# Cached-attention decode, two layers: eight instead of seven value quarters kept per row, and the first small loads issued by ScalarE

## The chip, the cores and the metric

The kernel runs on one core of a Trainium2 chip. The metric is the device time of one launch in microseconds (us). The engines are PE (TensorE: matmuls and transposes), DVE (VectorE), ACT (ScalarE), POOL (GpSimd) and SP (SyncE, which here only issues transfers). Sixteen DMA engines move data between HBM and the on-chip memory.

## The reference

Eight rows (one new token each) pass twice through attention over a long cache and an MLP. The weights and the cache are the same in both passes.

```python
# B = 8 rows, D = 448, 16 query heads on 8 cache heads, Sk = 4096, Dh = 256, bf16
def _A_ref(x, k_cache, v_cache, wq, wo):
    q = (x @ wq) split into heads
    k = jnp.repeat(k_cache, rep, axis=1)
    v = jnp.repeat(v_cache, rep, axis=1)
    scores = jnp.einsum("bhqd,bhkd->bhqk", q, k) * (Dh ** -0.5)
    p = _softmax(scores, axis=-1)
    o = jnp.einsum("bhqk,bhkd->bhqd", p, v)
    return heads of o side by side @ wo

def _B_ref(x, w1, w2, w3, w4):
    ...
    h2 = _gelu(_layernorm(x1, axis=-1) @ w3) @ w4
    return x1 + h2

x = A_x
x = x + _A_ref(_layernorm(x, axis=-1), A_k_cache, A_v_cache, A_wq, A_wo)
x = x + _B_ref(_layernorm(x, axis=-1), B_w1, B_w2, B_w3, B_w4)
x = x + _A_ref(_layernorm(x, axis=-1), A_k_cache, A_v_cache, A_wq, A_wo)
x = x + _B_ref(_layernorm(x, axis=-1), B_w1, B_w2, B_w3, B_w4)
```

The keys and the values of one row and one cache head are 4096 x 256 numbers of 2 bytes, 2 MiB each. All keys and values together are 268 MB, and each is used in both layers.

## The kernel before, in words

**The cache in quarters.** A head's 4096 positions are laid on 128 partitions, 32 positions on each. A *quarter* is a fourth of them: 8 positions a partition, 4096 bytes a partition, 512 KB. The tile `kv` (line 502) has room for 30 quarters (`QUARTERS`, line 14), its *slots*. A transfer brings one to four neighbouring quarters of one head into as many neighbouring free slots (`issue_kv`, line 640; the issue itself is line 646), so it has 512, 1024, 1536 or 2048 KB.

**What happens to a quarter.** Keys: PE transposes a quarter in two pieces into PSUM (line 1510), DVE or ACT copies each piece back over the slot (lines 1441 and 1442), and PE multiplies it with the queries, in one of two forms (lines 1149 and 1406). Values: PE multiplies the softmax weights with the quarter (line 1276, in `pv`), eight matmuls. The last reader of a slot carries `o.frees` (lines 1184, 1215, 1217 and 1298): only then may SP issue a transfer into that slot.

**What stays for the second layer.** Row by row, layer 0 of a row is followed by its MLP and by layer 1 of the same row, so a part of the row's keys and values can stay in the slots and is not loaded twice. `KEEP_K` (line 22) is 5: the keys of heads 3 to 6 stay whole, in 16 slots. Of head 7 (`HALF`) one quarter stays in a slot and the other three in PSUM banks and a side buffer (`hold` and `half_piece`). `KEEP_V` (line 23) is 7: the four value quarters of head 7 and quarters 1 to 3 of head 6 stay (`KEPT_V`, line 1102). So 24 slots of 30 are held at the most, and six go round. Heads 0, 1 and 2 are the *free heads*, of which nothing stays.

**The crossing.** This is the text's name for the stretch of a row in which all that is kept is held: from the last layer 0 load of the row (head 7's values) until layer 1 has scored the first kept keys, whose slots then come free. In it runs the chain of small steps that leads from one layer to the next: the output projection, the MLP, the normalisation and the new queries (`mid`, line 1540). Meanwhile SP loads the values of the next row's free heads, whose softmax weights are already there, as transfers of one quarter each (`MOST` = 1, line 39), and PE uses them up (lines 1688 and 1689 of the main loop). Behind them come values of layer 1's heads 6, 5 and 4.

**The order of the work.** Every step is recorded as an operation with an engine, an estimated duration and what it reads and writes (`Plan.op`, line 113). A planner (`Plan.schedule`, line 160) then fixes the order on every engine before anything runs. It assumes a latency of a transfer and a rate, chooses the slots and how many quarters go in one transfer (`next_kv`, line 206), puts filler matmuls (line 1719) where it sees PE idle, and so gives another order when a constant changes. SP issues strictly in its order: one transfer whose slot is not free holds up all behind it.

**The start.** `dma_once` (line 632) records transfers on SP. The rows `x_row` come first, then half of `wqx_sb` and half of `w3x_sb` (the last 64 rows of wq and of w3, folded on two halves of the partitions), then the first keys and wq. The other halves are issued on ACT's queue (lines 1576 and 1580). SP's place for a transfer is its last argument or `prio`; keys and values are numbered 0, 1, 2 and so on, so the numbers 0, 0.05 and 0.06 (times 4, less 0.5) stand ahead of all of them.

**The end.** The last value quarters are used by `pv_turned` (line 1286), and 28 columns of two rows pass the MLP (`last_rows`, line 948) to the last two output transfers (line 983).

Of the kernel before, what the change touches and what calls it, by code (L numbers as in the profile page):

```python
# [6 lines left out]
P = 128  # L7
B = 8
D = 448
# [10 lines left out]
RSQRT_STEPS = ((0.703952253, 1.681914091), (0.5, 1.5000003))  # L20
RSQRT_F = RSQRT_STEPS[1][0] * RSQRT_STEPS[0][0] ** 3
KEEP_K = 5
KEEP_V = 7
HOLD = 2
MARGIN4, MARGIN2 = 6, 2
REP = 24
# [450 lines left out]
def bass_interleave_layers__gqa_block_cached__mixer_s_mlp__decode_kernel(  # L477
# [20 lines left out]
    plan = Plan()  # L498
# [6 lines left out]
    def sb(name, shape, dt):  # L505
        n = 4 if dt in (f32, i32) else 2
        for s in shape[1:]:
            n *= s
        al = 32 if n >= 128 else 8
        cursor[0] = (cursor[0] + al - 1) // al * al  # L510
        t = nc.alloc_sbuf_tensor_at(name, shape, dt, offset=cursor[0], align_bytes=al)
        cursor[0] += (n + al - 1) // al * al
        assert cursor[0] <= high0, (name, cursor[0], high0)
        return t

    wq_sb = sb("wq_sb", [P, 3, 4096], bf)
    wqx_sb = sb("wqx_sb", [P, 2048], bf)
    wo_sb = sb("wo_sb", [P, 32 * D], bf)
    w3_sb = sb("w3_sb", [P, 3, F], bf)
    w3x_sb = sb("w3x_sb", [P, F // 2], bf)  # L520
# [40 lines left out]
    def over(name, shape, dt, at, skip=0):  # L561
        return nc.alloc_sbuf_tensor_at(name, shape, dt, offset=at.manual_sbuf_range[0] + skip)
# [13 lines left out]
    x_row = over("x_row", [B, NC5 * P], bf, w4_sb)  # L576
# [49 lines left out]
    def dma(name, dst, src, nbytes, sem, val, wr, at, row=8192):  # L626

        us = nbytes / 16 / 26.88e3 + nbytes / row / 16 * 0.008
        plan.op("sp", lambda eng: eng.dma_start(dst, src), us / FASTER, name, wr=wr, prio=at,  # L629
                dma=(sem, val))  # L630

    def dma_once(name, parts, keys, at, also=()):

        for i, (dst, src, nbytes, *row) in enumerate(parts):
            dma(name, dst, src, nbytes, nc.alloc_semaphore(f"s_{name}{i}"), 16,
                [keys[i], *(also if i == 0 else ())], 4 * at - 0.5, *row)
# [49 lines left out]
    def const_c(v):  # L686
# [7 lines left out]
            wr=["sel"])  # L694
# [7 lines left out]
    for bank, key in [(psR, "R"), (psM, M)]:  # L702
        plan.op("dve", lambda v, bank=bank: v.memset(bank[:, :], 0.0), 0.5, "const",
                wr=["psM", ("row", 0), ("row", 1)], banks=[key])
# [396 lines left out]
    lent = {}  # L1101
    KEPT_V = {HKV - 1 - i: range(max(4 * i + 4 - KEEP_V, 0), 4) for i in range((KEEP_V + 3) // 4)}
    done = {}
# [452 lines left out]
    def second_queries(b, h, prio):  # L1556
# [8 lines left out]
           rd=["psM", ("mom2", b), "cs_q"], wr=[("q2", b % 2, h)], banks=[M], prio=prio)  # L1565


    dma_once("x", [(x_row[:, 0:D], A_x[:, 0, :], 7168), (x_row[:, D + P:], A_x[:, 0, 3 * P:D], 1024)],
             ["xr0", "xr1"], 0)

    def load_wq():
        dma_once("wq", [(wq_sb[:, kc, :], A_wq[kc * P:(kc + 1) * P, :], 1 << 20)
                        for kc in range(3)], ["wq0", "wq1", "wq2"], 2)
        dma_once("wqx", [(wqx_sb[0:64, :], A_wq[384:D, 0:2048], 1 << 19)], ["wqx0"], 0.05)
        s_wqx = nc.alloc_semaphore("s_wqx1")
        plan.op("act", lambda a: a.dma_start(wqx_sb[64:P, :], A_wq[384:D, 2048:4096]), 0.1, "wqx1",
                wr=["wqx1"], prio=0, dma=(s_wqx, 16))
        dma_once("w3x", [(w3x_sb[0:64, :], B_w3[384:D, 0:896], 114688)], ["w3x0"], 0.06)
        s_w3x = nc.alloc_semaphore("s_w3x1")
        plan.op("act", lambda a: a.dma_start(w3x_sb[64:P, :], B_w3[384:D, 896:1792]), 0.1, "w3x1",  # L1580
                wr=["w3x1"], prio=1, dma=(s_w3x, 16))

    def load_rest():
        dma_once("wo", [(wo_sb[:, :].rearrange("p (t n) -> p t n", n=2 * D),
# [68 lines left out]
    def with_first_results(k, b):  # L1653
# [15 lines left out]
        run(k[MLP_TO:])  # L1669

    load_wq()
    load_rest()
    first_queries()
# [105 lines left out]
```

## Time and profile before

| | us |
|---|---|
| median of 3 runs | 1074.54 (1074.22 to 1076.17) |
| profiled execution | 1071.74 |
| its span, first to last instruction | 1069.8 |
| PE busy | 937.8 |
| DVE busy | 586.8 |
| ACT busy | 345.6 |

The mean granted PE clock is 0.954 of full speed. HBM read is 434.18 MB, 406 GB/s over the span. The profile's page cuts the span into 40 slices of 26.7 us and gives for each the busy share of every engine in tenths, the granted clock (PEclk), the busy share of the DMA engines (DMA) and the rate. A row of the batch takes about 128 us, so one crossing comes every five slices or so.

In a line such as `SPq L646 <- PE psP L1276` the queue of SP waited at the instruction of line 646 until PE had finished the one of line 1276 that writes the tile psP; the numbers are the sum of such waits, how many there were, and the longest. A line on DMA issues gives what is loaded from where, the number of issues, the size of each and the median time from issue to landing. A row of a table by stretches has the stretch, its length, and for each engine the busy time with the number of instructions, then the granted clock, the DMA share and the rate.

### The profile page before, as it was taken

To read this page: it belongs to the slowest core of one execution; us is meant where nothing else is said; L and a number is where in the kernel's file an instruction comes from. 1 tells how busy PE (TensorE), PEld (TensorE's weight loads), DVE (VectorE), ACT (ScalarE), POOL (GpSimd) and SP (SyncE) were. 2 spreads that over 40 slices of the span, in tenths; PEclk is the share of its full clock that TensorE was granted. 3 is DMA by queue.
4 is the path that set the end of the run, shared out by engine and by line. 5 is a ranking of instruction groups with operands and counts; after the bars stand their busy time and mean duration, and the time that the engine had idled before them with its cause. 6 is when DMAs were issued, how large, how long until landed. Compare 5 with 4: busy or idle time off the path is not lost.

```text
span 1069.8 us, 34153 instructions
## 1 busy us (share of the span) xinstructions
PE 937.8 (88%) x15215; PEld 650.7 (61%) x15215; DVE 586.8 (55%) x1879; ACT 345.6 (32%) x946; POOL 99.6 (9%) x284
## 2 busy tenths in 40 slices
PE   4889889998989989988898888898888998998896
PEld 4556556665556656666565565666656675666664
DVE  4345455555555556555565555565555665665464
ACT  1234113341334502354133431344223342253041
POOL 0000000010100101001010100101000000111011
PEclk9899999999999989999999999999999998999896
DMA  9999999999999999999999999999999999999995
GB/s 364 409 425 424 408 391 426 424 422 404 406 427 424 420 396 419 426 426 418 385 424 424 422 403 386 426 425 425 397 402 425 427 419 387 407 425 416 381 422 229
DMA packets 58110, 436.39 MB, mean 408 GB/s; under 512 B 6238, under 2 KB 9452, under 8 KB 35948
## 3 DMA queue, kind: packets, MB, share of 16 engines
q1 hardware_dynamic: 57796, 433.84, 98.6%
q8 instruction: 119, 1.95, 0.7%
q10 hardware_dynamic: 168, 0.38, 0.1%
q14 instruction: 27, 0.22, 0.1%
HBM read 434.18 MB, written 0.01 MB: 406 GB/s over the span
## 4 chain that ended last, share of the span: by engine, by line
DMA 56%; PE 36%; DVE 4%; issue 2%; SPq 1%; ACT 1%; POOL 0%
DMA kv<-in_A_k_cache_dram 30%; DMA kv<-in_A_v_cache_dram 26%; PE psT L1510 11%; PE psP L1276 8%; PE psT L1406 5%; PE psM L1149 3%; PE psM L902 2%; PE psR L1340 2%; PE psP L1719 1%; SPq L629 1%; PE psM L918 1%; DMA w_sb<-in_B_w_dram 1%; DVE oS L1304 1%; DVE oS L1302 1%; PE psP L1312 1%
## 5 line engine op out<-in xcount | busy, mean ns | idle before, releaser
L1510 PE MATMUL psT<-ident_f,kv 128*128 128x128 f32 x2752 | 372.7, 282 | 27.9 <-DMA kv<-in_A_k_cache_dram 26.2
L1510 PEld LDWEIGHTS psT<-ident_f,kv 128*128 128x128 f32 x2752 | 301.5, 143 | 107.6 <-issue 56.6
L1441 DVE COPY kv<-psT 128x512 f32<-128x512 f32 x364 | 250.4, 691 | 186.4 <-PE psT L1510 179.2
L1442 ACT COPY kv<-psT 128x512 f32<-128x512 f32 x356 | 207.9, 586 | 376.3 <-PE psT L1510 300.3
L1276 PE MATMUL psP<-kv,pT 128*2 128x256 bf16 x4032 | 170.9, 281 | 26.3 <-DMA kv<-in_A_v_cache_dram 24.3
L1406 PE MATMUL psT<-kv,qz 128*32 128x512 bf16 x1664 | 134.2, 396 | 3.8 <-ACT kv L1442 1.9
L1276 PEld LDWEIGHTS psP<-kv,pT 128*2 128x2 bf16 x4032 | 82.8, 82 | 68.8 <-DMA kv<-in_A_v_cache_dram 32.6
L1229 POOL PARTITION_ALL_REDUCE gm<-pm x128 | 45.4, 355 | 772.3 <-DVE pm L1227 762.2
L1239 ACT ACTIVATE pT<-sS,nb,fac 128x32 bf16<-128x32 bf16 x128 | 52.6, 417 | 122.7 <-DVE nb L1233 122.7
L1302 DVE CAST oS<-psP 128x256 bf16<-128x256 f32 x126 | 53.2, 422 | 51.0 <-PE psP L1276 49.9
L1340 PE MATMUL psR<-wo_sb,oT 128*1 128x448 bf16 x444 | 64.0, 372 | 7.7 <-DVE oT L1319 3.0
L1243 POOL PARTITION_ALL_REDUCE Db<-rs x128 | 51.0, 398 | 179.1 <-ACT pT L1239 179.1
L1719 PE MATMUL psP<-ident_f 128*128 128x256 bf16 x370 | 59.7, 288 | 0.0
L1312 PEld LDWEIGHTS psP<-sel,oS 128*128 128x128 bf16 x504 | 23.1, 98 | 60.1 <-DVE oS L1304 56.3
L1239 ACT ACTIVATE pT<-sS,nb 128x32 bf16<-128x32 bf16 x128 | 40.7, 326 | 54.7 <-DVE nb L1233 54.7
L1312 PE MATMUL psP<-sel,oS 128*128 128x2 bf16 x504 | 31.5, 166 | 30.2 <-DVE oS L1304 29.0
L1406 PEld LDWEIGHTS psT<-kv,qz 128*32 128x32 bf16 x1664 | 34.2, 95 | 37.3 <-issue 12.8
L1421 DVE CAST sr<-psT 128x512 bf16<-128x512 f32 x54 | 37.3, 691 | 33.5 <-PE psT L1406 33.4
L1304 DVE TENSOR_TENSOR oS<-psP,oS 128x256 bf16<-128x256 f32 x126 | 53.3, 423 | 2.8
L1149 PE MATMUL psM<-qz,kv 128*128 128x48 bf16 x1344 | 47.6, 186 | 6.4 <-issue 4.2
L1149 PEld LDWEIGHTS psM<-qz,kv 128*128 128x128 bf16 x1344 | 41.4, 99 | 17.2 <-issue 10.6
L1222 DVE CAST sS<-psM 128x64 bf16<-128x64 f32 x128 | 28.1, 219 | 41.3 <-PE psM L1149 28.4
(197 smaller groups left out, 796.5 us busy)
## 6 DMA issues: line engine op xcount, KB each, us to landing
kv<-in_A_k_cache_dram SPq DMA_DIRECT2D x66, 2048.0 KB, 23.2
kv<-in_A_v_cache_dram SPq DMA_DIRECT2D x61, 2048.0 KB, 17.3
kv<-in_A_v_cache_dram SPq DMA_DIRECT2D x174, 512.0 KB, 8.2
kv<-in_A_k_cache_dram SPq DMA_DIRECT2D x16, 1024.0 KB, 9.6
kv<-in_A_k_cache_dram SPq DMA_DIRECT2D x29, 512.0 KB, 9.0
kv<-in_A_k_cache_dram SPq DMA_DIRECT2D x9, 1536.0 KB, 17.4
kv<-in_A_v_cache_dram SPq DMA_DIRECT2D x13, 1024.0 KB, 9.2
kv<-in_A_v_cache_dram SPq DMA_DIRECT2D x4, 1536.0 KB, 11.0
```

The source lines that it names most:

```text
L1149: last = t.matmul(ps[:, SB + 2 * i:SB + 2 * i + 2 * REP], a()[:, c:256:2], bcast(rhs(c), REP, 1), start=(c == 0), stop=(c == 1))
L1239: return a.activation(pT[nr][:, :, :].rearrange("p i j -> p j i")[:, jj, :], sview[:, jj, :], ACT.Exp, bias=nb[nm][:, jj:jj + 1], scale=sc ...
L1276: last = t.matmul(ps[g4:g4 + 2, PV0:PV0 + DH], pT[nr][:, k, :], slot_ap(q, s * 256, 256), start=(i < 4), stop=(i >= 28), skip_group_check= ...
L1302: plan.op("dve", lambda v: v.tensor_copy(oS[:, 0, :], po), 0.36, "o", rd=[("pv", par, x) for x in range(4)], wr=["oS0"], banks=[bk], prio=hi)
L1304: plan.op("dve", lambda v: v.tensor_tensor(oS[:, 1, :], po, oS[:, 0, :], ALU.subtract), 0.36, "o", rd=["oS0"] + [("pv", par, x) for x in r ...
L1312: last = t.matmul(ps[:, PV1 + 2 * c:PV1 + 2 * c + 2], oS[:, w, c:DH:2], sel[:, :], start=(w == 0), stop=(w == 1))
L1340: last = t.matmul(psR[r:r + 1, 0:D], oT[no][:, i % 2, i // 2:i // 2 + 1], wo_sb[:, a:a + D], start=(k == 1 and i < 2), stop=(k == turn_at ...
L1406: last = t.matmul(psT[bank][32 * g:32 * g + 32, :], qz[:, a:a + 32], slot_ap(qs[g // 2], g % 2 * 1024, 1024)[:, c:1024:2], start=(half == ...
L1441: return e.tensor_copy(dst, psT[bank][:, :])
L1442: return e.copy(dst, psT[bank][:, :])
L1510: last = t.transpose(psT[bank][:, s * P:(s + 1) * P], src, ident_f[:, :])
L1719: return t.matmul(dst, ident_b, bcast(ident_b[:, 0:n // 4], 4, 1), start=True, stop=True)
```

## The change

`KEEP_V` becomes 8: quarter 0 of head 6's values stays too, so 25 slots are held at the most and five go round. `KEPT_V` follows from the constant, and the planner makes a new order of everything. Of the small first transfers, the two of `x_row` and the halves of `wqx_sb` and `w3x_sb` that SP issued are now issued on ACT's queue, by a helper `by_act`; all six stand there ahead of ACT's other work, and SP begins with the first keys.

```diff
-KEEP_V = 7
+KEEP_V = 8
...
-    dma_once("x", [(x_row[:, 0:D], A_x[:, 0, :], 7168), (x_row[:, D + P:], A_x[:, 0, 3 * P:D], 1024)],
-             ["xr0", "xr1"], 0)
+    def by_act(key, dst, src):
+
+        sem = nc.alloc_semaphore(f"s_{key}")
+        plan.op("act", lambda a: a.dma_start(dst, src), 0.1, key, wr=[key], prio=0, dma=(sem, 16))
+
+    by_act("xr0", x_row[:, 0:D], A_x[:, 0, :])
+    by_act("xr1", x_row[:, D + P:], A_x[:, 0, 3 * P:D])
 
     def load_wq():
         dma_once("wq", [(wq_sb[:, kc, :], A_wq[kc * P:(kc + 1) * P, :], 1 << 20)
                         for kc in range(3)], ["wq0", "wq1", "wq2"], 2)
-        dma_once("wqx", [(wqx_sb[0:64, :], A_wq[384:D, 0:2048], 1 << 19)], ["wqx0"], 0.05)
-        s_wqx = nc.alloc_semaphore("s_wqx1")
-        plan.op("act", lambda a: a.dma_start(wqx_sb[64:P, :], A_wq[384:D, 2048:4096]), 0.1, "wqx1",
-                wr=["wqx1"], prio=0, dma=(s_wqx, 16))
-        dma_once("w3x", [(w3x_sb[0:64, :], B_w3[384:D, 0:896], 114688)], ["w3x0"], 0.06)
-        s_w3x = nc.alloc_semaphore("s_w3x1")
-        plan.op("act", lambda a: a.dma_start(w3x_sb[64:P, :], B_w3[384:D, 896:1792]), 0.1, "w3x1",
-                wr=["w3x1"], prio=1, dma=(s_w3x, 16))
+        by_act("wqx1", wqx_sb[64:P, :], A_wq[384:D, 2048:4096])
+        by_act("wqx0", wqx_sb[0:64, :], A_wq[384:D, 0:2048])
+        by_act("w3x0", w3x_sb[0:64, :], B_w3[384:D, 0:896])
+        by_act("w3x1", w3x_sb[64:P, :], B_w3[384:D, 896:1792])
```

## The prediction

> **What bounds the kernel now.** I read the page's slices first, then what the SyncE queue waits for, then single transfers in the trace.
>
> ```profile
> span 1069.8 us, 34153 instructions
> PE 937.8 (88%) x15215; PEld 650.7 (61%) x15215; DVE 586.8 (55%) x1879; ACT 345.6 (32%) x946; POOL 99.6 (9%) x284
> DMA  9999999999999999999999999999999999999995
> GB/s 364 409 425 424 408 391 426 424 422 404 406 427 424 420 396 419 426 426 418 385 424 424 422 403 386 426 425 425 397 402 425 427 419 387 407 425 416 381 422 229
> DMA packets 58110, 436.39 MB, mean 408 GB/s; under 512 B 6238, under 2 KB 9452, under 8 KB 35948
> ```
>
> The DMA engines are busy in every slice but the last, while PE, the busiest compute engine, has 12% to spare. The rate is 424 to 427 GB/s in good slices and 381 to 408 once per row: that dip is the crossing.
>
> ```profile
> kv<-in_A_k_cache_dram SPq DMA_DIRECT2D x66, 2048.0 KB, 23.2
> kv<-in_A_v_cache_dram SPq DMA_DIRECT2D x61, 2048.0 KB, 17.3
> kv<-in_A_v_cache_dram SPq DMA_DIRECT2D x174, 512.0 KB, 8.2
> ```
>
> Landings, read one by one, are evenly spaced: the median step is 4.90 us for a 2048 KB transfer, 3.72 for 1536, 2.49 for 1024, 1.27 for 512. A latency of 23.2 us for 4.9 us of data says that several wait in line. So the time is the sum of these steps, plus the start, plus 9.85 us behind the last landing (1059.95), which the change leaves alone: the last four transfers are single quarters of values before and after.
>
> ```profile
> core 0: us, PE busy (x) PEld busy (x) DVE busy (x) ACT busy (x) POOL busy (x), PEclk, DMA share, GB/s
> 257.20:272.20 15.00, 12.41 (x330) 8.73 (x331) 7.62 (x45) 0.21 (x1) 0.00 (x0) 1.00 1.02 387
> 290.00:300.00 10.00, 9.12 (x172) 6.46 (x161) 5.54 (x19) 3.41 (x11) 1.11 (x3) 1.00 1.01 426
> ```
>
> The upper stretch is row 1's crossing: six free quarters go round, one 512 KB transfer each. The DMA share is full there too, so six are enough; the lower rate is mostly the worse step of a quarter (4 x 1.27 = 5.08 against 4.90) and instruction fetches (119 packets, 1.95 MB over the span).
>
> **The change, part by part.**
>
> *Bytes.* Head 6's quarter 0 of values is no longer loaded a second time: one quarter in each of 8 rows, 4.19 MB. The built program shows 448 value quarters against 456. The order planner also groups the rest anew; cache transfers of 2048, 1536, 1024 and 512 KB go from 127, 13, 29 and 203 to 130, 12, 35 and 174. At the steps above that is 622.3 + 48.4 + 72.2 + 257.8 = 1000.7 us before and 637.0 + 44.6 + 87.2 + 221.0 = 989.8 after: **-10.9 us**.
>
> *Start.* Six small transfers now stand on ACT's queue, and the first keys are SP's first.
>
> ```profile
> 0.72 0.75 SPq L629 DMA_DIRECT2D x_row<-in_A_x_dram  x2
> 1.51 0.56 SPq L629 DMA_DIRECT2D wqx_sb<-in_A_wq_dram  x1
> 2.12 0.73 SPq L629 DMA_DIRECT2D w3x_sb<-in_B_w_dram  x1
> 2.89 1.24 SPq L646 DMA_DIRECT2D kv<-in_A_k_cache_dram  x2
> ```
>
> The keys are issued 2.89 - 0.72 = 2.17 us sooner; that is the most to be won. The 736 KB of wqx and w3x still have to move, now between the keys' packets; from their packets (128 of 4096 B at 145 ns where nothing slows them, 128 of 1792 B at about 85 ns, over 16 engines) that is 1.16 + 0.68 = 1.84 us, so the least is 2.17 - 1.84 = 0.33. Before, those packets took 2.0 to 5.0 us of the clock at about 240 GB/s, since some took 170 to 420 ns; part of this is hidden among key packets. I take the middle, **-1.3 us**. The Trainium skill (DMA: Bandwidth & Descriptors, "Issuing engines are not separate DMA queues") says that queues of several engines share the same 16 DMA engines and that spreading saves issue time alone. By it the term is 0.33 and the sum 1 us worse; the trace before cannot show this.
>
> ACT issues four more transfers of about 0.6 us, all ahead of its table load (1.97 us now) and its first copy at 16.03, before which it idles 12.78 us: nothing. x_row must land before the first transposes (4.69); it stands first on its queue, and the queries need wq's third part anyway (landed 25.49), so wqx may come late by 10 us. Without that cover each us of delay would move the first queries by as much, while the transfers already issued still give SP's queue some 13 us of work at its first blocked issue (46.09 against 59.48).
>
> *Five quarters instead of six.* Between the last kept load of a row and layer 1's first key scores, 17 key and 7 value quarters are held of 30; now 25. The next row's free-head values go round in what is left. A reload waits for the PE (line 1291's product, o.frees) that read the quarter, and SP issues in order, so every later transfer waits with it, and then PE for all of them.
>
> ```profile
> SPq L646 <- PE psP L1276: 499.5, 152, 25.7
> SPq L646 <- PE psT L1406: 231.9, 50, 17.8
> SPq L646 <- PE psM L1149: 66.0, 29, 5.0
> ```
>
> These waits cost nothing as long as enough transfers are in flight. What counts is the line ahead at an issue: landing of the transfer before it, minus the issue. Its least value in each row's crossing, rows 0 to 7, is 4.83, 5.23, 4.81, 4.54, 4.92, 4.51, 4.66, 4.64 us. With a quarter less I subtract 1.27: 3.56, 3.96, 3.54, 3.27, 3.65, 3.24, 3.39, 3.37. A gap opens when this is below the time from issue to the start of the transfer's own step. That need is not shown directly; bounds:
> - 1024 KB issued at 151.40 had 3.05 us ahead and landed after 6.48, so its step began after 6.48 - 2.49 = 3.99: the need is at most that.
> - The V quarter at 518.04 had 4.54 ahead and landed after 5.81 without a gap; the K quarter at 791.30 had 4.51 and lost 0.32. So 4.54 is safe for a quarter.
> - ACT's first 256 KB, into an idle queue, landed after 3.63; less 0.64 of its own, 2.99.
>
> ```profile
> L646 SPq DMA_DIRECT2D kv<-in_A_k_cache_dram x1: 328/328/328, 151.4 to 151.4; - x1
> ...
> DMA to landing us min/median/max: 6.5/6.5/6.5
> ```
>
> The shortfalls add up to 0 at a need of 2.99, 0.43 + 0.03 + 0.45 + 0.72 + 0.34 + 0.75 + 0.60 + 0.62 = 3.9 us at 3.99, and 8 x 4.54 - 27.98 = 8.3 at 4.54. I take 3.99, the shallowest row there is: **+3.9 us**. The Trainium skill has a DMA fit in the same page (DMA: Bandwidth & Descriptors, "Anatomy of one DMA — SWDGE (gpsimd) path": about 2.0 us plus bytes at 436 GB/s, for GpSimd's path) would make a quarter land in 3.2 us and the loss 0; the 6.48 us for 1024 KB, against its 4.4, speaks against taking it here.
>
> The far side of the crossing is covered: from the landing of head 7's values to the first reload that waits for a layer 1 score, rows 0 to 5 took 15.66, 15.08, 14.94, 14.49, 14.30 and 13.79 us, the latency of the MLP and the queries. Before, 16 or 17 quarters (20.4 us) could be issued without it; now 15 or 16 (19.1 to 20.4), less 3.99 of need 15.1 and more. Only row 0 (19.3 - 3.99 = 15.3) comes short, by 0.4, inside its shortfall above.
>
> **Sum.** -10.9 - 1.3 + 3.9 = -8.3 us. The profiled execution took 1071.74 us (span 1069.8), 2.8 below the median of runs, 1074.54. I apply it to both: profiled 1063.4 with a span of 1061.5, median **1066.2**. With the ends of the terms: -10.9 - 2.2 + 0 = -13.1, 1061.4; and -10.9 - 0.3 + 8.3 = -2.9, 1071.6.
>
> **Rivals.**
>
> 1. *The turn is hidden* (need about 3): -10.9 - 1.3 = -12.2, **1062.3**. For it: the idle-queue row, and PE consumes most quarters 0.5 to 1.0 us after landing in rows 1, 4 and 5. Against it: 3.99 at 151.40. The fit of the Trainium skill named above would come out here.
> 2. *The round trip takes over* and it is slower. Place: the ten reloads of each crossing that now have four quarters behind their predecessor's use (4 x 1.27 + 1.27 = 6.35 us for landing, PE, issue, landing; 7.64 before). If the step begins 5.50 us after issue, as for the quarter at 996.43 (4.74 ahead, 0.76 lost), the shortfalls are 8 x 5.50 - 27.98 = 16.0 and the time is 1074.5 - 10.9 - 1.3 + 16.0 = **1078.3**. It decides from 12.2 us of loss, a need of (12.2 + 27.98)/8 = 5.02. For it: row 2, where the clock fell to 0.62 and PE gave quarters back only after 1.6 to 2.1 us; shortfalls could also recur in the second round. Against it: 4.54 sufficed at 518.04, and such losses stand at instruction-fetch packets as well.
> 3. *It gives nearly all back*: a need of 4.8 to 5.2 loses 10.4 to 13.6, **1074** or so. Evidence as for 2.
> 4. *The quarter is not really saved*: excluded by the built program's count; PE taking over would need more than its 12% idle.
>
> **How the numbers follow.** Forecast (need 3.2 to 4.8, faster): 0.56; rival 1: 0.23; rival 3: 0.09; rival 2: 0.12. A measurement of this kernel tells 0.2%, 2.1 us, from no change. Faster: 0.56 + 0.23 = 0.79; same 0.09; slower 0.12. The likeliest case's own range is 1061.4 to 1071.6; to leave out 2 in 10 I take 1061 to 1074.
>
> **What would show it.** Bytes: HBM read 4.19 MB less, 174 quarters. Start: the first key transfer issued near 0.7 and landing one to two us before 12.27. Turn: in each crossing a landing step or two of 1.4 to 2 us instead of 1.27 and PE waiting there for the values' DMA, a DMA share just below full, 3 to 5 us over the rows. It is wrong if those gaps pass 1.5 us a row, if the need shown by short lines is under 3.2 or over 4.8, or if quiet slices lose their 425 GB/s.

## The result, and the profile after

| | before | changed |
|---|---|---|
| median of six runs, us | 1074.07 (1072.47 to 1076.17) | 1080.84 (1079.46 to 1082.29) |
| profiled execution, us | 1071.74 | 1079.71 |
| its span, us | 1069.8 | 1077.9 |

The changed kernel takes 1.0059 times as long, with an interval of 1.0044 to 1.0074: 6.3 us slower, where 8.3 us faster was forecast. First the page of the changed kernel, the lines that answer to those of the prediction.

```profile
span 1077.9 us, 34068 instructions
PE 937.0 (87%) x15188; PEld 650.2 (60%) x15188; DVE 596.5 (55%) x1890; ACT 336.8 (31%) x935; POOL 99.7 (9%) x284
DMA  9999999999999999999999999999999999999995
GB/s 316 409 428 421 410 363 424 425 424 392 402 424 426 419 361 395 425 426 422 378 422 426 422 417 355 426 426 425 396 392 426 426 419 369 388 423 418 329 424 223
HBM read 429.99 MB, written 0.01 MB: 399 GB/s over the span
kv<-in_A_k_cache_dram SPq DMA_DIRECT2D x68, 2048.0 KB, 22.6
kv<-in_A_v_cache_dram SPq DMA_DIRECT2D x62, 2048.0 KB, 17.6
kv<-in_A_v_cache_dram SPq DMA_DIRECT2D x146, 512.0 KB, 7.2
```

The line of the kernel before that answers to the one on HBM:

```profile
HBM read 434.18 MB, written 0.01 MB: 406 GB/s over the span
```

Three things are to be seen. HBM read fell from 434.18 to 429.99 MB, just the 4.19 MB that were to be saved. The good slices still run at 424 to 428 GB/s, so the time was lost elsewhere: the first slice has 316 GB/s for 364, and the slice of a crossing has 329 to 396 where it had 381 to 408 (the slices don't fall on the same work in both). The busy digits are still 9 in every slice but the last. They can't show this loss; the rates do. And the median from issue to landing of a 512 KB value transfer fell from 8.2 to 7.2 us: one transfer less, 1.27 us, is in line ahead of it.

The start, by the timeline of the changed kernel (start, duration, engine, line; the SP queue, then the ACT queue, then PE):

```profile
0.72 0.87 SPq L646 DMA_DIRECT2D kv<-in_A_k_cache_dram  x2
...
0.72 0.92 ACTq L1571 DMA_DIRECT2D x_row<-in_A_x_dram  x2
1.67 1.21 ACTq L1571 DMA_DIRECT2D wqx_sb<-in_A_wq_dram  x2
2.91 1.32 ACTq L1571 DMA_DIRECT2D w3x_sb<-in_B_w_dram  x2
...
7.64 0.27 PE L1601 MATMUL psM<-ident_f,x_row 8*128 8x8 bf16 x5 [7.64 <-DMA x_row<-in_A_x_dram]
```

The keys are issued 2.17 us sooner, as the diff says. Their first transfer lands 0.95 us sooner (11.32 for 12.27), but everything behind it lands later: wqx's last half at 18.00, w3x's at 22.30, wq's third part at 28.81 (25.49 before), and wo, the weight of the output projection and the last one in this stretch, at 57.96 (54.59). So the start has lost 3.4 us by wo. The stretches from 8 to 16 us, before and then after:

```profile
8.00:16.00 8.00, 3.69 (x18) 3.69 (x19) 2.79 (x8) 0.00 (x0) 0.00 (x0) 1.00 0.99 422
```

```profile
8.00:16.00 8.00, 5.76 (x58) 5.68 (x59) 5.45 (x24) 0.00 (x0) 0.00 (x0) 1.00 1.01 277
```

The DMA share is 1 in both, the rate 422 and 277 GB/s. At 277 these 8 us moved what 5.25 us move at 422: 2.75 us of the 3.4 stand here. Both queues had packets in this stretch, and a 16 KB packet took 940 ns in the median, against 614 in the same stretch before, where SP's transfers were alone.

The crossings. These rows of the changed kernel by stretches are row 1's crossing, a good stretch behind it, and the crossing of the last row:

```profile
260.10:275.10 15.00, 13.15 (x308) 8.63 (x301) 7.96 (x45) 0.21 (x1) 0.00 (x0) 0.69 0.96 354
295.00:305.00 10.00, 8.79 (x158) 6.31 (x150) 6.46 (x20) 2.92 (x11) 1.11 (x3) 1.00 1.02 429
1003.30:1012.00 8.70, 7.44 (x175) 5.02 (x168) 4.85 (x25) 0.21 (x1) 0.00 (x0) 0.69 0.85 283
```

Row 1's crossing fell from 387 to 354 GB/s, and in the last row the DMA share shows it too, 0.85. The waits of SP's queue (sum, times, longest) look much as before, and would mislead: 466.9 us for 499.5 at the values' product.

```profile
SPq L646 <- PE psP L1276: 466.9, 130, 26.1
SPq L646 <- PE psT L1406: 241.8, 49, 18.4
SPq L646 <- PE psM L1149: 85.9, 41, 6.6
```

What counts is the prediction's line ahead. I took it for every transfer from its issue and the landing of the one before, and as its loss the time from that landing to its own, less its normal step. In the trace before, 16 cache transfers had under 5 us ahead; after, 57 have. Transfers with under 6 us ahead lost 9.2 us together before and 25.0 after. From the landing of row 0's head 7 values to the last landing of all, the kernel took 936.47 us before and 941.24 after: 4.8 more, though the steps are 10.9 shorter. So 15.6 us were lost there, where the prediction had 3.9. With 3.4 of the start, 8.1 is the difference of the spans; behind the last landing nothing changed (9.82 and 9.81 us). These are two single executions, and the one before is a short one (1071.74 us, where the median is 1074.07); so the 15.6 may be one or two us too much.

### The profile page after: what moved, and what is told of

Same layout as the page of the kernel before. It is cut to its first block, busy times and chain, and to the rows that moved or that the text cites. A ratio compares the mean times of both kernels' runs of the same rounds, so it can differ in the third digit from the quotient of the medians.

```text
span 1077.9 us, 34068 instructions
## 1 busy us (share of the span) xinstructions
PE 937.0 (87%) x15188; PEld 650.2 (60%) x15188; DVE 596.5 (55%) x1890; ACT 336.8 (31%) x935; POOL 99.7 (9%) x284
## 3 DMA queue, kind: packets, MB, share of 16 engines
HBM read 429.99 MB, written 0.01 MB: 399 GB/s over the span
## 4 chain that ended last, share of the span: by engine, by line
DMA 63%; PE 31%; DVE 3%; issue 1%; ACT 1%; SPq 0%; POOL 0%
DMA kv<-in_A_v_cache_dram 32%; DMA kv<-in_A_k_cache_dram 32%; PE psT L1510 10%; PE psP L1276 7%; PE psT L1406 4%; PE psM L1149 2%; PE psM L902 1%; PE psR L1340 1%; PE psM L918 1%; DVE oS L1304 1%; DVE oS L1302 1%; PE psP L1720 1%; PE psM L1066 1%; PE psP L1312 0%; PE psM L1432 0%
## 5 line engine op out<-in xcount | busy, mean ns | idle before, releaser
L1510 PE MATMUL psT<-ident_f,kv 128*128 128x128 f32 x2752 | 376.8, 283 | 30.9 <-DMA kv<-in_A_k_cache_dram 28.8
L1441 DVE COPY kv<-psT 128x512 f32<-128x512 f32 x377 | 258.8, 691 | 191.1 <-PE psT L1510 183.0
L1442 ACT COPY kv<-psT 128x512 f32<-128x512 f32 x343 | 200.1, 586 | 391.0 <-PE psT L1510 310.1
L1276 PE MATMUL psP<-kv,pT 128*2 128x256 bf16 x4032 | 167.9, 281 | 32.5 <-DMA kv<-in_A_v_cache_dram 29.8
L1406 PE MATMUL psT<-kv,qz 128*32 128x512 bf16 x1664 | 132.0, 395 | 3.6 <-ACT kv L1442 1.5
L1421 DVE CAST sr<-psT 128x512 bf16<-128x512 f32 x58 | 40.1, 691 | 29.7 <-PE psT L1406 29.5
L1720 PE MATMUL psP<-ident_f 128*128 128x256 bf16 x341 | 55.6, 288 | 0.0
```

Source lines behind the costliest of these rows:

```text
L1276: last = t.matmul(ps[g4:g4 + 2, PV0:PV0 + DH], pT[nr][:, k, :], slot_ap(q, s * 256, 256), start=(i < 4), stop=(i >= 28), skip_group_check= ...
L1406: last = t.matmul(psT[bank][32 * g:32 * g + 32, :], qz[:, a:a + 32], slot_ap(qs[g // 2], g % 2 * 1024, 1024)[:, c:1024:2], start=(half == ...
L1441: return e.tensor_copy(dst, psT[bank][:, :])
L1442: return e.copy(dst, psT[bank][:, :])
L1510: last = t.transpose(psT[bank][:, s * P:(s + 1) * P], src, ident_f[:, :])
L1720: return t.matmul(dst, ident_b, bcast(ident_b[:, 0:n // 4], 4, 1), start=True, stop=True)
```

## The experiments

Twelve kernels, each compared with runs of the kernel before on the same chip. The first four ask which part of the change costs what.

**The start alone** (the changed kernel with seven quarters kept).

```diff
-KEEP_V = 8
+KEEP_V = 7
```

> The six small loads on ACT's queue as in the change, but seven value quarters kept. Theory (two parts that add up; the start costs because two queues with work share the same DMA engines and each packet takes longer then): slower than before by about 3.4 us, the amount by which wo's landing came later in the changed kernel (57.96 against 54.59 us); 1077.5, wo landing near 58, crossings as before. Rival (the start only matters together with the fewer free quarters, or is caught up later): within 1 us of before.

1079.29 us (1077.97 to 1081.20) against 1075.09, 1.0045 (1.0030 to 1.0060): 4.8 us slower, where about 3.4 were expected. In its trace wo lands at 57.19, 2.6 us late, and the stretch from 8 to 16 us is slow as in the changed kernel; 16 KB packets take 856 ns there.

```profile
8.00:16.00 8.00, 6.60 (x73) 6.11 (x69) 6.40 (x25) 0.31 (x1) 0.00 (x0) 1.00 1.02 303
```

So the new start by itself is a loss. Some 2 of the 4.8 us stand behind wo, in later rows, whose order the planner made anew. The reloads of its crossings lost some 2 us more than those of the trace before, but the other kernels with six going round differ among themselves by more than that, so where the 2 us come from stays open.

**The quarter alone** (the kernel before with eight kept).

```diff
-KEEP_V = 7
+KEEP_V = 8
```

> Eight value quarters kept, the start as before. Theory: the byte saving of 10.9 us is there, and the reloads of the crossing give back 15 to 16 us, so slower than before by about 4 to 5 us, 1078 to 1079, with wo landing at 54.6. Rival (the start is the whole loss, the kept quarter pays): faster than before by about 7 us, 1067.

1076.60 us (1072.24 to 1082.88, ten runs), 1.0014 (0.9989 to 1.0039): 1.5 us slower, not told from nothing. The prediction's terms for this part give a gain of 7.0; the expectation, a loss of 4 to 5, was too dark as well. Its profiled execution is the longest of the ten, so its trace serves for no sum. Together with the start alone, 4.8 + 1.5 = 6.3 us: the change is the sum of its two halves, as far as these are known, to 2 or 3 us each.

**Five going round, and no byte saved** (the kernel before with a slot less).

```diff
-QUARTERS = 30
+QUARTERS = 29
```

> The kernel before with room for 29 quarters instead of 30: seven value quarters kept, the same bytes as before, but five quarters go round. Theory (depth alone, five in flight do not cover the time from issue to landing): slower than before by 13 to 17 us, 1087 to 1091, with gaps at reloads that have less than 5 us of line ahead. Rival (the loss hangs on head 6's values staying whole, on the new grouping of transfers, or on the layer change's chain of small steps): within 4 us of before.

1086.88 us (1082.73 to 1093.23), 1.0119 (1.0081 to 1.0158): 12.8 us slower by the ratio (its interval is 8.7 to 17 us), 11.8 by the medians, a little under the 13 to 17 that were expected. The bytes are those of before. Its page, and row 1's crossing with a good stretch behind it:

```profile
span 1080.9 us, 34114 instructions
...
HBM read 434.18 MB, written 0.01 MB: 402 GB/s over the span
```

```profile
257.00:272.00 15.00, 14.34 (x358) 9.99 (x361) 7.93 (x46) 0.80 (x2) 0.18 (x1) 0.79 0.98 357
290.00:300.00 10.00, 8.10 (x135) 5.68 (x132) 6.00 (x20) 2.97 (x10) 1.51 (x4) 1.00 1.02 429
```

357 GB/s in the crossing as in the changed kernel (354), 429 outside it. So the sixth quarter in the round is worth some 12 us, a little more than the saved bytes, and with -10.9 for these it accounts for the 1.5 of the kernel above.

**One queue for the start** (the kernel before, with wqx and w3x on SP behind the first two key transfers).

```diff
-        dma_once("wqx", [(wqx_sb[0:64, :], A_wq[384:D, 0:2048], 1 << 19)], ["wqx0"], 0.05)
-        s_wqx = nc.alloc_semaphore("s_wqx1")
-        plan.op("act", lambda a: a.dma_start(wqx_sb[64:P, :], A_wq[384:D, 2048:4096]), 0.1, "wqx1",
-                wr=["wqx1"], prio=0, dma=(s_wqx, 16))
+        dma_once("wqx", [(wqx_sb[64:P, :], A_wq[384:D, 2048:4096], 1 << 18),
+                         (wqx_sb[0:64, :], A_wq[384:D, 0:2048], 1 << 18)], ["wqx1", "wqx0"], 1.97)
...
```

(w3x in the same way at 1.98.)

> The kernel before with all four halves of wqx and w3x on SP's queue behind the first two key transfers, none on ACT's: one queue, the same transfers. Theory (interleaving of two queues is what slows the packets): no slow stretch at the start, 16 KB packets at about 614 ns, wo landing 0.5 to 2 us sooner than 54.59, the time 1073 to 1074. Rival (the 64-row transfers are slow in themselves, wherever they stand): wo landing at 57 to 58 as in the change, 1077.

1075.49 us (1072.22 to 1077.33, ten runs), 1.0003 (0.9990 to 1.0017): no difference. The first keys land at 8.95, 3.3 us sooner, but wo at 55.55, 0.97 later, so the expectation of an earlier wo failed, and that of the rival, 57 to 58, too. Packets of 16 KB stay at 611 to 614 ns: the same transfers one behind the other don't slow them, on two queues at once they did. Whether any two queues would do so, or only small packets among the large ones, no run separates. The small packets are slow also on the one queue: 254 ns in the mean for 4096 B and 133 for 1792 B, where the cache's packets of 4096 B and w4's of 1792 B take 159 and 76 in the median. Then wqx and w3x cost 128 x 254 / 16 + 128 x 133 / 16 = 3.1 us of all sixteen engines, not the 1.84 of the prediction. The stretches:

```profile
8.00:16.00 8.00, 7.01 (x38) 6.87 (x39) 4.23 (x7) 1.10 (x2) 0.00 (x0) 1.00 0.99 349
15.00:19.00 4.00, 3.52 (x29) 2.77 (x27) 2.77 (x4) 1.76 (x3) 0.00 (x0) 1.00 1.04 317
```

The next four vary what is kept and what goes round.

**Seven going round** (the kernel before with six kept; 8 quarters more to load).

```diff
-KEEP_V = 7
+KEEP_V = 6
```

> Six value quarters kept, the start as before, room for 30: seven quarters go round and eight quarters more are loaded. Theory (bytes cost their steps, and beyond six in flight nothing more is won): transfers sum to 1009.4 us against 1000.7, so 8 to 11 us slower than before less at most 3 us of losses that six still have: 1080 to 1086. Rival (the crossing goes on gaining from a seventh quarter as it did from the sixth, 12 us): 1072 to 1075, no slower than before.

1080.58 us (1079.77 to 1082.29), 1.0052 (1.0037 to 1.0067): 5.6 us slower. The steps of its transfers add up to 1009.4 us for 1000.7, so a seventh quarter in the round wins back some 3 us, far less than the sixth.

**29 slots and six kept** (six go round as in the kernel before, 8 quarters more to load).

```diff
-QUARTERS = 30
+QUARTERS = 29
...
-KEEP_V = 7
+KEEP_V = 6
```

> Room for 29 quarters and six value quarters kept: six go round as before, eight quarters more are loaded. Theory: slower than before by the steps alone, 1010.8 against 1000.7 us, 9 to 12 us, 1084 to 1087; the crossings lose no more than before. Rival (room as such costs, wherever it is taken): slower by 15 us or more.

1084.99 us (1084.20 to 1086.75), 1.0089 (1.0072 to 1.0105): 9.6 us slower. With the round left alone, a quarter a row is worth about what its bytes are.

**Room made by leaving a weight out**, with 30 slots and with 31. Both leave out the loads of w3 and w3x, and the MLP reads w4's bytes in their place, so their output isn't the reference's. The second has 31 slots and keeps eight, and six still go round. The part of the edit that both share, without the loads:

```diff
-    w3_sb = sb("w3_sb", [P, 3, F], bf)
-    w3x_sb = sb("w3x_sb", [P, F // 2], bf)
...
-                w = w3_sb[:, kc, mt // 7 * 896:mt // 7 * 896 + 896][:, c] if kc < 3 else w3x_sb[:, c]
+                o = kc * F + mt // 7 * 896 if kc < 3 else 3 * F
+                w = w4_sb[:, o:o + 896][:, c]
...
```

> The kernel before without the loads of w3 (1.6 MB, 3.9 us of steps); the first MLP product reads w4's bytes in its place, so the output is not the reference's. Room for 30 quarters, seven values kept, six go round. It is the partner of the next kernel, on the same freed memory. Both theories: 3 to 5 us faster than before, 1070 to 1072.

> As the partner without w3's loads, but the freed memory gives a 31st quarter, and eight value quarters are kept: six go round again, and the saved quarter is saved. Theory (bytes pay their steps as long as six are in flight): transfers sum to 990.2 us against the partner's 1000.3, so 9 to 11 us faster than the partner, 1060 to 1062. Rival (keeping head 6's values whole, or the new grouping of transfers, is itself what costs): within 4 us of the partner.

The first took 1074.51 us (1073.39 to 1080.65, ten runs), 1.0011 (0.9993 to 1.0030): no gain, where 3 to 5 us were expected. wo lands 4.5 us nearer to row 0's last values, but from there to row 1's last values it takes 136.31 us for 131.41. Probably that is because w4, which the MLP now needs first, is loaded later than w3 was (landed at 127.76, w3 at 118.53); this is not shown. The second took 1067.06 us (1064.51 to 1068.85), 0.9922 (0.9904 to 0.9941); the 1060 to 1062 expected had the missing gain of its partner in it. Against its partner that is 0.9922 / 1.0011, 9.6 us less: the eighth quarter pays for its bytes where the round keeps six.

The last four carry this over to a kernel that leaves nothing out. The tiles began at byte 16512 of each partition. The 16 KiB below are what the Trainium skill (SBUF — State Buffer, "SBUF size: 192, 224, or 256?") calls the scratch for the descriptors of GpSimd's transfers. No run here shows what it is used for; but every transfer of this kernel in the traces is issued by SP or ACT, and the size is an argument where the program is made.

```diff
-QUARTERS = 30
+QUARTERS = 31
...
-KEEP_V = 7
+KEEP_V = 8
...
-    cursor = [16512]
+    cursor = [4224]
...
-    nc = _bacc.Bacc("TRN2", target_bir_lowering=False, num_devices=1)
+    nc = _bacc.Bacc("TRN2", target_bir_lowering=False, num_devices=1,
+                    dynamic_dma_scratch_size=4096)
```

**31 slots, eight kept** (the diff above), and **33 slots, ten kept** (the same with 33 and 10):

> The start as before, eight value quarters kept, and a 31st quarter of room, which comes from 12 KB per partition of on-chip memory that was set aside for descriptors of GpSimd's transfers (this kernel has none); nothing is left out. Theory (the saved bytes pay their steps as long as six quarters go round): transfers sum to 989.5 us against 1000.7, so 9 to 12 us faster than before, 1063 to 1066. Rival (keeping head 6's values whole costs by itself): within 4 us of before.

> The same with all of these 12 KB: room for 33 quarters, ten value quarters kept, six go round. Theory: transfers sum to 970.1 us against 1000.7, so 27 to 33 us faster than before, 1042 to 1048. Rival (beside the bytes something else bounds the crossing, such as PE's work or the chain of small steps): at most 20 us faster.

1063.52 us (1061.25 to 1065.70), 0.9889 (0.9865 to 0.9913), 12 us faster; and 1042.98 us (1042.31 to 1045.46), 0.9696 (0.9674 to 0.9719), 32.6 us faster, with steps 30.6 us shorter. The first one's page has the changed kernel's bytes in 16 us less:

```profile
span 1061.9 us, 34012 instructions
...
HBM read 429.99 MB, written 0.01 MB: 405 GB/s over the span
```

**34 slots with eleven kept, and with twelve** (the same edit with 34, and with 11 and 12; a size of 32 bytes, the first tile at byte 160). The first has six going round, the second five.

> All 16 KB of the set-aside memory used: room for 34 quarters, eleven value quarters kept, six go round, the start as before. Theory: transfers sum to 960.4 us against 1000.7, so 36 to 43 us faster than before, 1032 to 1039. Rival (another bound shows): at most 34 us faster, no better than room for 33 with ten kept.

> The step of the change once more, from eleven kept quarters with six going round to twelve with five: room for 34 quarters, the start as before. Theory (a quarter less in flight gives back what the saved quarter saves): transfers sum to 949.8 us, 10.6 less than the partner's, and the reloads lose 11 to 14 us more; within 4 us of the partner. Rival (the loss in the first case hung on head 6's values or on 30 quarters): 8 us or more faster than the partner.

1036.26 us (1034.91 to 1038.04), 0.9645 (0.9594 to 0.9697), about 37 us faster, the best of all; and 1037.56 us (1033.25 to 1039.98), 0.9648 (0.9582 to 0.9714), the same. The pages of the two, eleven first:

```profile
span 1035.3 us, 33890 instructions
...
GB/s 360 406 428 419 411 363 411 426 423 415 402 425 424 422 390 402 425 425 424 372 421 427 425 419 395 410 425 423 416 379 425 425 421 401 411 424 417 373 422 181
...
HBM read 417.41 MB, written 0.01 MB: 403 GB/s over the span
```

```profile
span 1036.6 us, 33907 instructions
...
GB/s 363 406 429 422 409 379 427 424 423 403 391 424 425 425 369 410 427 425 421 364 414 424 425 414 312 422 424 425 403 368 427 425 421 371 403 427 412 333 421 191
...
HBM read 413.21 MB, written 0.01 MB: 399 GB/s over the span
```

This is the change's own step, from six to five, tried once more: 4.20 MB less read, and no time won, since the crossings' slices go down to 312 and 333 GB/s. Its some 75 reloads with four other quarters between them and the last landing in their slot lose 15.5 us; the some 70 of the kernel with eleven, with five between, lose 5.3. The difference, 10.2, is about the 10.6 that the steps are shorter.

## Why the prediction was wrong

**Bytes, -10.9: right.** The issues and the bytes came out as counted. A quarter a row without a change to the round measured 9.6 us (29 slots and six kept), 9.6 (31 against 30 slots without w3) and 12 (31 slots, nothing left out).

**Start, -1.3: the wrong sign.** The trace shows +3.4 by wo, and the start alone +4.8 in the whole kernel. The step that failed is "part of this is hidden among key packets". More was lost than anything hidden could have won: while both queues have packets, those of each take longer, 856 and 940 ns for 614 at 16 KB, 221 and 213 for 159 at 4096 B on ACT's queue. The size of 1.84 us was also too small, 3.1 by the kernel with one queue. Its 145 ns for 4096 B is a misreading: no packet of that size took less than 156 ns in the trace. And the first transfer's landing was the wrong thing to watch: 0.95 us sooner there, 3.4 later at the end of the start. The Trainium skill's rule that the prediction weighed (DMA: Bandwidth & Descriptors, "Issuing engines are not separate DMA queues") agrees in that nothing beyond issue time was saved. The 0.33 us of gain that the prediction worked out for that case was still too good, since the start lost time.

**Five going round, +3.9, at most 8.3: the place was right, the size three to four times too small.** The kernel with a slot less measures some 12 us, and the changed trace 15.6. The step that failed is the sum of "its least value in each row's crossing": one shortfall per row, against one fixed need. The reloads with only four quarters between them and their slot's last landing were 2 before and are some 75 now, nine or ten in a crossing, and they lose all along it: 17.5 us together, 0.23 each (19 lose over 0.2). The some 75 reloads of the trace before that had five between lost 3.3 to 3.6, 0.05 each. The difference, some 14 us, is nearly all of the 15.6. A quarter goes round by landing, use on PE, reissue and landing again. (The product that gives a slot back is that of line 1276, as the lines on waits show; the prediction's line 1291 is used at the end only.)

In the changed trace the size of a loss goes with the time from a quarter's landing to the reissue of its slot: under 0.6 us some 28 reloads lose 0.05 each; 0.6 to 1.1, 27 lose 0.24; 1.1 to 2, 17 lose 0.33; over 2, 3 lose 1.34. These times are like those of before (mean 0.98 and 0.93 us), but there 1.27 us more of data covered them, and up to 2 us of such time the loss was 0.03 to 0.04. The worst stands in the last row. PE by the timeline of the changed kernel (start, duration; the last bracket is idle time and what ended it):

```profile
1004.75 0.25 PE L1312 MATMUL psP<-sel,oS 128*128 128x2 bf16 x4 [1.26 <-DVE oS L1304]
1004.87 1.67 PE L1066 MATMUL psM<-hT,w_sb 128*128 128x28 bf16 x55
...
1006.61 0.58 PE L1066 MATMUL psM<-hT,w_sb 128*128 128x28 bf16 x14
1007.11 0.91 PE L1340 MATMUL psR<-wo_sb,oT 128*1 128x448 bf16 x4
1007.96 0.27 PE L773 MATMUL psM<-x2c 128*128 128x3 bf16 x4
1008.15 0.60 PE L1276 MATMUL psP<-kv,pT 128*2 128x256 bf16 x8
```

A value quarter had landed at 1004.10 and the next at 1005.39, but PE first does the MLP's matmuls and the output projection that stand ahead in its order. The first quarter's product begins at 1008.15, and its slot is reissued at 1008.79, 4.69 us after its landing.

**"4.54 is safe": wrong.** One quarter with 4.54 ahead and no gap was one case. In the changed trace transfers with 4 to 4.5 us ahead lose 0.44 on average (22 of them), with 4.5 to 5, 0.16 (27); single ones with 4.76 and 4.43 ahead began their step 5.68 and 5.97 us after issue. Nor is the need fixed the other way: the quarter issued at 1008.79 with 1.53 ahead landed 4.12 us later, so its step began by 2.85. The trace before had the warning in it: its 14 quarters with 4.5 to 5 us ahead lost 0.19 on average. An estimate from these, 75 reloads at 0.19 less the 3.3 to 3.6 that they lost before, gives some 11 us, near the measured 12. Why a quarter needs 2.85 once and almost 6 another time isn't settled. Uneven progress of the sixteen engines would fit, but the trace doesn't name the engine of a packet. Fetches of instructions among the packets are not what sets the losing reloads apart: in the changed trace one falls into the step of 8 of the 19 that lose over 0.2, and of 23 of the 58 others.

**The rivals.** The second, the round trip taking over, is what came: 16.0 us was its loss, 15.6 the trace's and some 12 that of the timed kernel with a slot less. It had the ten reloads of a crossing that matter and said that shortfalls could recur, and was given 0.12 on the ground of that one transfer at 518.04. Its fixed need of 5.50 is not what the traces show, and its 1078.3 us has a gain at the start where there was a loss, so its price came near partly by luck. The first, a turn that is hidden, falls. The estimate by the Trainium skill's fit for GpSimd's path (DMA: Bandwidth & Descriptors, "Anatomy of one DMA — SWDGE (gpsimd) path"), 3.2 us for a quarter, is below the shortest landing of one in any trace here, 3.83 us in the kernel with the quarter alone, whose transfers SP issues. The third would have been right without the start's loss: the quarter alone gave back all that it saved. The fourth was rightly excluded.

**What it called free.** PE did not become the bound (937.0 us busy for 937.8). ACT's four more issues cost ACT nothing that shows: its table load comes at 4.25, long before its first copy at 17.27, before which it idles 11.73 us. The end is unchanged. The first transposes waited 2.95 us longer for x_row (7.64 for 4.69); what of the 2 us in later rows comes from that isn't known.

**The sum.** By the timed runs: +4.8 for the start and +1.5 for the quarter, +6.3 us, which is what was measured. The 1.5 is -10.9 for the bytes, by their steps, and so +12.4 for the round; the kernel with a slot less, measured apart, has 11.8 to 12.8 for it.

## What to carry to other kernels

Where slots go round through landing, use and reissue, price one slot fewer by the loss of every transfer in the round, and take the loss from all transfers of the trace with a short line ahead, not from the single one that got through; the simplest test is to take the slot away without the gain that pays for it. Room for more slots is better looked for outside the round: 16 KB per partition that no transfer here used were worth 37 us. Moving small loads to a second queue did not hide them here, and the first landing doesn't tell what a start is worth; take the landing of the last weight in it.

## What the runs showed of the hardware

- Small loads on ACT's queue at the same time as the keys on SP's cost throughput: 277 and 303 GB/s from 8 to 16 us, against 422 for the same 8 us of the kernel before; a 16 KB packet takes 856 to 940 ns for 614. Whether two queues alone do this, or the small packets, isn't known.
- Packets of the transfers that fill only 64 partitions are slow even on one queue: 254 ns in the mean for 4096 B, against 159 in the median for the cache's packets of that size. Not all are: the first such transfer of the kernel before, with nothing ahead of it, has 159 in the median (216 in the mean). No run here shows why.
- Reloads of 512 KB with six going round lost 0.04 to 0.11 us each in nine kernels, with five 0.15 to 0.29 in four, while the DMA busy digits stay at 9 or 8 in every slice but the last.
